# Normaliser rows stored as sixteen DRAM rows, with the step order, evacuation engines and buffers drawn up again

## Chip, cores and metric

The kernel runs on one core of a Trainium2 chip. The metric is the device time of one execution in microseconds; the figure for the kernel before is the median of three runs. The core has five engines with queues of their own: PE (matmul), DVE (vector), ACT (scalar and activation), POOL and SP, and 16 DMA engines that move data between DRAM and the on-chip memories.

## What is computed

Four residual layers over a sequence of 2048 rows of width 512 with 32 heads of 16: A, B, A, B, each on a layer-normalised copy of x. Both A layers use the same weights, and so do both B layers. Layer A is linear attention with a softmax feature map, layer B a sliding window of eight keys at distance two.

```python
def _A_ref(x, wqkv, w_phi, wo):
    qkv = ((x @ wqkv).reshape(B, S, 3, H, Dh)).transpose(2, 0, 3, 1, 4)
    q, k, v = qkv[0], qkv[1], qkv[2]
    pq = einsum("bhsd,hdf->bhsf", q, w_phi); pk = einsum("bhsd,hdf->bhsf", k, w_phi)
    phi_q = concat([softmax(pq), softmax(-pq)]); phi_k = concat([softmax(pk), softmax(-pk)])
    kv = einsum("bhsf,bhsd->bhfd", phi_k, v); z = einsum("bhsf->bhf", phi_k)
    o = einsum("bhqf,bhfd->bhqd", phi_q, kv) / (einsum("bhqf,bhf->bhq", phi_q, z)[..., None] + 1e-6)
    return merge_heads(o) @ wo
def _B_ref(x, wqkv, wo):
    # each query sees positions s, s-2, ..., s-14 (masked below 0)
    logits = einsum("bhsd,bhswd->bhsw", q, kg) * Dh ** -0.5
    o = einsum("bhsw,bhswd->bhsd", softmax(logits), vg)
    return merge_heads(o) @ wo
x = x + A(ln(x)); x = x + B(ln(x)); x = x + A(ln(x)); x = x + B(ln(x))
```

## The kernel before

The sequence is cut into four blocks of 512 rows (b = 0 to 3), each of four tiles of 128 rows. x stays on chip. For each of the two rounds L = 0, 1 and each block there is a chain of stages, and each stage is a method that registers small steps on named threads, one thread for each stage and engine.

- `s_loads`, `s_fold`, `s_ln_first`: loads of x and weights; w_phi is folded into the q and k parts of the A weights by transposes and matmuls whose PSUM results are copied into WA (`ev`, `ev2`); the first layer norm.
- `s_a1` (k and v of layer A): k projection on PE (L616 and L628 are the k and v matmuls), exponentials Ek on ACT (L622), sums and their reciprocal (t8 to t1 and `rr`), multiplication on DVE (L674), then `kv`, which adds up all blocks' key-value products in one PSUM bank.
- `s_a2` (q of layer A): projection (L721), exponentials Eq (L729), their sums S and 1/S.
- `s_akv`: the barrier. It needs the `kv` of all four blocks; it copies the sum to kvT and builds the matrices ZM and R from it.
- `s_a3`: the denominator from ZM and Eq, then the normaliser rho, a [128, 2, 128] tile that holds, for 4 tiles x 32 heads on the partitions, the two signs and 128 rows. rho must be spread over the 16 features of each head and multiplied into Eq. For four of the eight (round, block) pairs, (0,2), (0,3), (1,2) and (1,3), this goes through DRAM: `wr` stores rho (L847), `rdb` reads it back with repetition into Prho (L854), `muld` multiplies (L858). For the others PE spreads it (`bc`), and DVE multiplies from PSUM or from a bf16 copy that ACT makes (`bev`, L869; `mulp`, L839).
- `s_a4`: output of layer A and its projection; `s_out` adds the residual either on DVE (L556) or by an identity matmul on PE (L546) with a copy on ACT (L553), and does the sums and the layer norm that follows (L563, L575, L450 to L468; transposes by PE or by DMA, L473).
- `s_b1` to `s_b3` (layer B): projections (L950), `prod` of q and the shifted keys on DVE (L1042), head sums on PE (`lgt`, L1049), exponentials, sums and their reciprocal (`ex`, `den`, `rd`), the weights PT (L1077), the gathered v (`vrep`, DMAs Vg from V, L1011), `pav` on DVE (L1104), sums on PE (L1113) and the output projection (L543). The pair (1,3) takes another form of layer B, `s_e0` to `s_e4`, with its scores and outputs on PE (L1277, L1321, L1365), a mask product (L1303) and a normalisation oB on DVE (L1348).

The order of all steps on every engine is written out in three tables. `_ORDER` lists the threads in the order in which their next step is issued (base 36 numbers of thread names), 1488 entries; an engine executes its own steps in that order and waits by semaphores. `_CHOICE` has one digit for each movable step (an evacuation from PSUM, a normalisation, a residual add, a bf16 copy of spread rho): 1 is DVE and 0 is ACT, except that for a residual add 1 is PE with ACT, and for the copy of rho 1 means that there is none. `_SLOTS` says which buffer each tile takes: 16 medium ones, 8 PSUM banks, 8 large ones (Ek, prod, pav, Vg and others share them), 6 small ones.

```python
def copy(self, dve, out, in_):
    if dve:
        self.nc.vector.tensor_copy(out=out, in_=in_)   # L203
    else:
        self.nc.scalar.copy(out=out, in_=in_)          # L205
```

Of the kernel before, what the change touches and what calls it, by code (L numbers as in the profile page):

```python
# [8 lines left out]
BF16 = mybir.dt.bfloat16  # L9
# [7 lines left out]
P = 128  # L17
# [57 lines left out]
6k 6m 7s 6k 6n 6c 4v 69 6k 94 95 4x 96 97 6o 69 4x 6f 6i 98 6f 3h 6j 7t 7u 7w 6a 6e 6r 6r 6r 99 9a 99 99 9b 9c
9b 99 9d 9b 9e 6r 9b 9f 7y 7z 6q 6q 9b 83 9f 84 9j 6s 6s 9i 9g 6s 6s 88 6t 6t 9h 7y 80 b2 6s 6t 88 88 8b 4x 8a
6q 4x 4y 4y 7y 81 89 83 85 7y 8d 82 8f 6r 6u 9k 83 3h 4w 4x 9r 9s 9r 6u 6u 6q 4y 7x 88 9r 86 9t 9u 8c 9r 9v 6v
6w 6v 6u 6x 6v 6y 6v 9m 6z 70 70 9n 71 72 4w 73 70 70 83 74 9w 4v 72 72 4z 75 4z 72 50 4v 8e 50 51 8e 4z 50 53
4z 50 76 8f 72 52 76 54 79 9x 8f 87 9m 9m 55 55 55 55 7a 78 8f 77 7b 9o 56 57 8e 9w 9w 5a 9w 7x 58 57 9p 59 57
57 a1 a3 5b 9z 9y a3 57 5b 5e 5c 8g 8g 8g 8g a3 9m 9q 8h 8h 5f b3 b3 8e b3 a3 b4 5d 5g b6 8g 9l 8h b3 8f 8i bz  # L80
bz a4 a4 b5 a4 a4 b0 a0 a2 b7 a2 c0 c0 a5 a5 b1 b1 c0 c0 bz c0 b0 b1 a4 bx bx bx as as b1 by a5 at by by 8j by
8i 8j 8l 8i 8j 8m ar 8k 8i 8j 8n b0 b0 b1 8o a2 ap b1 8o 8o b1 b1 c0 a3 a6 by by 8p 8q a6 a6 8o 8r 8q 8s 8t ap
as 8q 8q 8u 8q a2 a6 8u 8w bz 8x ap a7 aq aq av a7 8y au a7 a8 b8 8v a7 b8 b8 a9 aa ap ab ac ac ac af ac c0 c0
ad as bx ag aq aq aq aq aq aq ae aw ah 8z bb bb b8 b9 bb by by ax be ax be b8 ae ae ae ai ae be be bc ai bc bc
aj ac ak ac am an ac ac bo bc bc ax ax ay bc al bb ao bc bm bn ax bc bj bm bn bn bn bm bn bn bp bu bu bu bu bq
bm bn bp bv bn br bg bj az az az az ba bj bj bu bk bz bu c0 bp bp bh c1 c1 c2 ba ba bf ba bj bl bl bu bu c1 c1
bl bu bi bl bw bs bt bw c2 bv bu bw bw c2 c2 c2 c2 c2 bx c7 c8 c9 c2 c1 c9 c9 ca fp by cb c2 cc cb c3 c4 c4 fq
fr ca cd c3 cg ce cb cb fq fs cf cb ca cj ch c3 c3 ci e0 c4 c4 cb cb cb cb ck cb c4 cl c4 c4 c4 e1 e2 cm cn e1
c3 c4 co e0 cp h9 e3 e1 ha e4 fs e1 cq e5 e1 e0 e8 e6 cq cq cr e9 cs e1 e7 e1 ea e1 e1 e1 hb ha fs cu hc ct cs
eb ee ed ec cs cq cv cs ef eg eh eg eg fq cw fq ft cs cw cy cx eg fu d1 fw cq cq cz ek d0 cq cq fv fx el fy fz  # L90
d2 ei ej ei ei ei em ei em eo fy hc eq ha ep df df df di df en da hc db dj ha dh dg d4 d5 dk d6 dl d5 d5 d8 hd
hg fy fy g3 da hf he hh hi da d7 dc hi hi da hi g2 g0 g1 dl g0 er g0 g0 hl g4 g0 dd hj ey ey ey hk hk hm de f8
ez dl et et hn g4 g6 f3 g5 hk d5 hk ho hk eu ho hq f3 hr et hp f3 dk hs dk g8 dk d9 f3 fa g7 f0 dl ev f1 f7 fa
f6 et f4 ey f5 f2 dm dm ew dm dm dn fb dn ht fb ex fa es i1 i2 i1 g9 i1 i4 dl dm i3 dn i1 i5 gl gl fb gn fa fb
i7 i9 i9 fc fc i9 id i9 fb gm ib fc ie f9 dl f9 gb gb ia gd hw hx c6 i6 do hu hu do do dp hv dq do gc dp i6 dp
dp i8 dt i6 i6 i6 gg i6 hw hw hz hy i6 i6 dr gb ge ds gg hw gi c6 i0 i6 i6 i6 i6 gg gj gg fa fd gk fe ff i6 i6
i6 i6 fd fe fg i7 if ig ic gh es ic ic gb f9 gf gq gs gs gs if ig if f9 if gl ig ig gl gp if if gt gt go ig ig
c5 c5 c5 gs gt gt gu gu if ig ih if ig ic ic ic ic ic du du dv ic gt gu du fd fd fe ih ih ih ic ic fh gs ic ic
# [14 lines left out]
_SLOTS = {  # L113
    "med": (
        "0123456789abcdef246559a55b68d5574c29efa8d2e9a857ef290d974caee2587fbd20897a5ecd5ddfbcee2dc7e456fb9a08"
        "e452d6f08c7ba4931e5fd62ca4"
    ),
    "ps": (
        "0123012456173526017417230146127631426134256126712307634256021304150236710245306712314025346710345267"
        "3012304562314023425671472345360123452102356174206345062306236231021341203145012301234524350123105423"  # L120
        "0452046312430567462306420316301452374523045014236570571057105270340123102345670123401567023451014265"
        "3012450120345670345012316750231720325674016237645701521342042042413510432034501256123120104523012020"
        "31220123012451302412"
    ),
    "big": (
        "012345670123451234567134056713052671054263754213675420137541036752034672046703154"
    ),
    "t2": (
        "0123455555555500112344444444444444444405012321222222224514031000010100011100002253333441000000000000"
        "000000025234113051"  # L130
    ),
    "pp": (
        "462462064646"
    ),
}

# [1 line left out]
class _Fast:  # L138
# [655 lines left out]
    def s_a3(self, L, b, dma):  # L794
        nc, add = self.nc, self.step
        st = "a3_%d%d" % (L, b)
        zm = self.ZM[L]
        T = {}
# [42 lines left out]
        pitch = (16 + _OPT["rho_pad"]) * P  # L841

        def wr():
            self.RD[L, b] = rd = self.dram.tile([8, 2, pitch], BF16, name="rd%d%d" % (L, b))
            a = rd[0:1, 0, 0:P]
            dst = bass.AP(a.tensor, a.offset, [[P, 16], [2 * pitch, 8], [pitch, 2], [1, P]])
            nc.sync.dma_start(out=dst, in_=T["rho"][:])  # L847

        def rdb(s):
            rd = self.RD[L, b]  # L850
            T["P", s] = pr = self.med([4, NB, P], "Prho")
            a = rd[0:1, s, 0:P]
            src = bass.AP(a.tensor, a.offset, [[2 * pitch, 8], [0, 16], [1, 16 * P]])
            nc.sync.dma_start(out=pr[:].rearrange("p t a i -> p (t a i)"), in_=src)  # L854

        def muld(s):
# [1243 lines left out]
```

## Time and profile before

| What | Value |
|---|---|
| Median of the runs (lowest to highest) | 333.31 us (331.84 to 334.52) |
| The profiled execution's own time | 333.73 us |
| Its span, first to last instruction | 332.0 us |
| Mean granted TensorE clock | 0.989 |
| Busy PE, DVE, ACT, POOL | 311.0, 291.6, 280.6, 42.0 us |
| HBM read and written | 11.13 MB, 2.99 MB |

The profile is of one execution. Busy time is the time in which an engine had an instruction in work; a row that groups instructions gives their number, their joint busy time and the mean duration of one, and after a second bar the idle time just before them with what ended it. Since instructions of one engine overlap a little, joint busy time over the number is less than the mean duration, and it is what one more instruction adds. A releaser in angle brackets is the work that ended a wait. "SPq" rows are DMA issues: the time is how long SP was held, not how long the data took.

### The profile page before, as it was taken

To read this page: it belongs to the slowest core of one execution; us is meant where nothing else is said; L and a number is where in the kernel's file an instruction comes from. 1 tells how busy PE (TensorE), PEld (TensorE's weight loads), DVE (VectorE), ACT (ScalarE), POOL (GpSimd) and SP (SyncE) were. 2 spreads that over 40 slices of the span, in tenths; PEclk is the share of its full clock that TensorE was granted. 3 is DMA by queue.
4 is the path that set the end of the run, shared out by engine and by line. 5 is a ranking of instruction groups with operands and counts; after the bars stand their busy time and mean duration, and the time that the engine had idled before them with its cause. 6 is when DMAs were issued, how large, how long until landed. Compare 5 with 4: busy or idle time off the path is not lost.

```text
span 332.0 us, 8893 instructions
## 1 busy us (share of the span) xinstructions
PE 311.0 (94%) x3551; PEld 153.6 (46%) x3577; DVE 291.6 (88%) x445; ACT 280.6 (85%) x648; POOL 42.0 (13%) x64
## 2 busy tenths in 40 slices
PE   8999999999999999899999999889999999996991
PEld 3654546445454443444443445644544444443540
DVE  5998996978999889999998899699699999998762
ACT  4899999998779998899999999999989858794640
POOL 7000000000205001040000000000001259440000
PEclk9999999999999999999999999999999999998997
DMA  7946200023889999569973000033399962779642
GB/s 201 363 116 126 88 0 4 2 60 88 162 130 157 132 163 146 85 120 159 140 100 58 8 2 4 4 88 103 84 119 149 183 141 51 186 132 158 112 160 72
DMA packets 44640, 36.14 MB, mean 109 GB/s; under 512 B 29680, under 2 KB 39984, under 8 KB 44592
## 3 DMA queue, kind: packets, MB, share of 16 engines
q1 hardware_dynamic: 44064, 35.48, 57.1%
q8 instruction: 30, 0.49, 0.7%
q14 instruction: 18, 0.15, 0.2%
q10 hardware_dynamic: 528, 0.02, 0.1%
HBM read 11.13 MB, written 2.99 MB: 43 GB/s over the span
## 4 chain that ended last, share of the span: by engine, by line
PE 33%; ACT 21%; DVE 12%; DMA 7%; issue 5%; SPq 1%; ACTq 0%; DVEq 0%
PE PS L950 13%; PE PS L543 7%; ACT Eq L729 5%; ACT sqd L563 4%; DMA Prho<-rd 3%; ACT Ek L622 3%; DVE prod L1042 3%; PE PS L1049 3%; PE PS L1170 2%; DVE pav L1104 2%; PE PS L1113 2%; DMA xnT<-xn 2%; DMA Vg<-V 2%; DVE Ek L674 2%; ACT oT L205 2%
## 5 line engine op out<-in xcount | busy, mean ns | idle before, releaser
L950 PE MATMUL PS<-xnT,WB 128*128 128x512 bf16 x336 | 77.3, 380 | 0.7 <-DVE QT L203 0.3
L1104 DVE TENSOR_TENSOR pav<-PT,Vg 128x4096 bf16<-128x4096 bf16 (+1 forms) x29 | 63.3, 2215 | 3.3 <-DMA Vg<-V 2.5
L1042 DVE TENSOR_TENSOR prod<-QT,K 128x4096 bf16<-128x4096 bf16 x28 | 63.2, 2286 | 0.3
L950 PEld LDWEIGHTS <-WB 128*128 128x128 bf16 x336 | 37.2, 114 | 37.5 <-issue 4.6
L543 PEld LDWEIGHTS <-oT 128*128 128x128 bf16 x240 | 22.4, 99 | 31.7 <-issue 6.2
L622 ACT ACTIVATE Ek<-PS 128x512 bf16<-128x512 f32 x64 | 34.0, 627 | 0.4 <-issue 0.4
L729 ACT ACTIVATE Eq<-PS 128x512 bf16<-128x512 f32 x64 | 34.2, 622 | 0.0
L563 ACT ACTIVATE sqd<-x 128x512 bf16<-128x512 bf16 x48 | 30.4, 634 | 3.9 <-DVE x L556 2.7
L992 POOL COPY vh<-V 128x64 bf16<-128x64 bf16 x6 | 9.6, 1592 | 180.4 <-ACT V L205 153.2
L543 PE MATMUL PS<-WoB,oT 128*128 128x512 bf16 x107 | 28.4, 390 | 3.6 <-issue 3.2
L205 ACT CAST oT<-PS 128x512 bf16<-128x512 f32 (+1 forms) x50 | 27.1, 594 | 4.7 <-PE PS L1113 4.6
L721 PE MATMUL PS<-xnT,WA 128*128 128x512 bf16 x128 | 30.6, 380 | 0.3 <-DVE Eq L839 0.3
L628 PE MATMUL PS<-WA,xnT 128*128 128x512 bf16 x123 | 30.5, 379 | 0.3
L543 PE MATMUL PS<-WoA,oT 128*128 128x512 bf16 x120 | 30.2, 379 | 0.5 <-issue 0.2
L616 PE MATMUL PS<-WA,xnT 128*128 128x512 bf16 x123 | 30.2, 379 | 0.3
L556 DVE SCALAR_TENSOR_TENSOR x<-PS,x 128x512 bf16<-128x512 f32 x42 | 27.2, 684 | 3.1 <-PE PS L543 2.9
L205 ACT CAST K<-PS 128x512 bf16<-128x512 f32 x31 | 17.6, 595 | 2.3 <-PE PS L1170 1.9
L628 PEld LDWEIGHTS <-xnT 128*128 128x128 bf16 x128 | 12.4, 98 | 14.7 <-issue 0.4
L674 DVE TENSOR_TENSOR Ek<-Ek,rk 128x4096 bf16<-128x4096 bf16 (+1 forms) x10 | 18.6, 1860 | 0.6 <-ACT rk L669 0.6
L616 PEld LDWEIGHTS <-xnT 128*128 128x128 bf16 x128 | 12.1, 98 | 15.1 <-issue 1.6
L553 ACT ACTIVATE x<-PS 128x512 bf16<-128x512 f32 x22 | 13.1, 601 | 6.5 <-PE PS L546 6.3
L721 PEld LDWEIGHTS <-WA 128*128 128x128 bf16 x128 | 11.8, 98 | 14.3 <-issue 0.6
(163 smaller groups left out, 509.9 us busy)
## 6 DMA issues: line engine op xcount, KB each, us to landing
Vg<-V SPq DMA_DIRECT2D x112, 131.5 KB, 5.7
Prho<-rd SPq DMA_DIRECT2D x8, 512.0 KB
x<-in_A_x_dram SPq DMA_DIRECT2D x3, 512.0 KB
WB<-in_B_wqkv_dram SPq DMA_DIRECT2D x3, 512.0 KB, 8.1
out_dram<-x SPq DMA_DIRECT2D x6, 256.0 KB, 3.1
wraw<-in_A_wqkv_dram SPq DMA_DIRECT2D x4, 256.0 KB
vd<-Vs SPq DMA_DIRECT2D x2, 272.0 KB, 4.3
x<-in_A_x_dram SPq DMA_DIRECT2D x4, 128.0 KB, 3.7
```

Source lines behind the costliest of these rows:

```text
L205: self.nc.scalar.copy(out=out, in_=in_)
L543: nc.tensor.matmul(y[:], lhsT=lh(t, c), rhs=Wo()[:, c, :], start=(c == 0), stop=(c == NB - 1 and not onpe))
L556: nc.vector.scalar_tensor_tensor(out=xb[:, t, :], in0=T[t][:], scalar=1.0, in1=xb[:, t, :], op0=ALU.mult, op1=ALU.add, **kw)
L563: nc.scalar.activation(out=sqd[:], in_=xb[:, t, :], func=ACT.Square, accum_out=T["ss"][:, t:t + 1])
L616: nc.tensor.matmul(pk[:], lhsT=xnT[:, t, k, :], rhs=self.WA[:, k, D:2 * D], start=(k == 0), stop=(k == NB - 1))
L622: nc.scalar.activation(out=T["E"][:, t, s, :], in_=T["k", t][:], func=ACT.Exp, scale=1.0 - 2.0 * s)
L628: nc.tensor.matmul(pv[:], lhsT=xnT[:, t, k, :], rhs=self.WA[:, k, 2 * D:3 * D], start=(k == 0), stop=(k == NB - 1))
L721: nc.tensor.matmul(pq[:], lhsT=self.WA[:, k, hb * P:(hb + 1) * P], rhs=xnT[:, :, k, :], start=(k == 0), stop=(k == NB - 1))
L729: nc.scalar.activation(out=self.Eq[L, b][s][:, :, hb, :], in_=T[hb][:].rearrange("p (t i) -> p t i", t=4), func=ACT.Exp, scale=1.0 - 2.0 * s)
L950: nc.tensor.matmul(pp[:], lhsT=self.WB[:, k, i * D + c:(i + 1) * D:NB], rhs=xnT[:, :, k, :], start=(k == 0), stop=(k == NB - 1))
L1042: nc.vector.tensor_tensor(out=pr[:], in0=QT[:, c:c + 1, :].to_broadcast([P, NW, TB]), in1=win, op=ALU.mult)
L1104: nc.vector.tensor_tensor(out=pv, in0=PT[:, :, lo:lo + n].unsqueeze(1).to_broadcast([P, NB, 2, n]), in1=vw, op=ALU.mult)
```

## The change

The code changes in one place, the stores and reads of rho. `wr` lays rho out in sixteen DRAM rows instead of eight, each of the two signs by a DMA of its own, and each value is stored in two rows; `rdb` reads sixteen rows, each eight times, where it read eight rows, each sixteen times.

```diff
         pitch = (16 + _OPT["rho_pad"]) * P
 
         def wr():
-            self.RD[L, b] = rd = self.dram.tile([8, 2, pitch], BF16, name="rd%d%d" % (L, b))
-            a = rd[0:1, 0, 0:P]
-            dst = bass.AP(a.tensor, a.offset, [[P, 16], [2 * pitch, 8], [pitch, 2], [1, P]])
-            nc.sync.dma_start(out=dst, in_=T["rho"][:])
+            self.RD[L, b] = rd = self.dram.tile([16, 2, pitch], BF16, name="rd%d%d" % (L, b))
+            for s in range(2):
+                a = rd[0:1, s, 0:P]
+                dst = bass.AP(a.tensor, a.offset, [[P, 16], [4 * pitch, 8], [2 * pitch, 2], [1, P]])
+                nc.sync.dma_start(out=dst, in_=T["rho"][:, s, :].unsqueeze(1).to_broadcast([P, 2, P]))
 
         def rdb(s):
             rd = self.RD[L, b]
             T["P", s] = pr = self.med([4, NB, P], "Prho")
             a = rd[0:1, s, 0:P]
-            src = bass.AP(a.tensor, a.offset, [[2 * pitch, 8], [0, 16], [1, 16 * P]])
+            src = bass.AP(a.tensor, a.offset, [[2 * pitch, 16], [0, 8], [1, 16 * P]])
             nc.sync.dma_start(out=pr[:].rearrange("p t a i -> p (t a i)"), in_=src)
 
         def muld(s):
```

The three tables are new. `_CHOICE` keeps the number of ones (120 of 380), at other places:

```diff
 _CHOICE = (
-    "1110110111101101111010000001100000000011000000101011111111101000001001110000000000000000100110101100"
-    "0001010100001111000000000000000011110001000000000111100000000000000011000111000000011011000000000000"
-    "1000000011111100000000000000110110100110110110111101000000000000000001010110011011001110001110100000"
-    "00000000011111010000011010000100000000000000000000000000010000011000000000001100"
+    "0010110111100111111111000000100000100110011100000111011110010100000101010000100000000000111101011100"
+    "1010010100001100100000000000000011111110000100001010100000000000000000010111001000001101000000000000"
+    "1010000011111100000000000100010110011011010100101111000000001001000000010110010001000100011100100000"
+    "00000000011111010000011100000000000000000000000001000011001000000000000000001100"
 )
```

Counted by kind, with the number on DVE before and after: evacuations of v in layer A 6 and 8, of layer A's output 10 and 12, of the key-value sum 0 and 1 (of 2), of layer B's projections 5 and 6, of the halo of k in the last block 0 and 1, of layer B's output 1 and 2, of first transposes 3 and 1; residual adds of layer A on DVE 26 and 29 (the rest on PE and ACT, 6 and 3); rho products straight from PSUM 21 and 18 of 32; normalisations 46 and 46 of 64.

`_ORDER` is another permutation of the same 1488 entries. Its first line before and after:

```diff
-4e d3 2 8 9 a b 0 d4 j 0 k i i i i i i 1m 1n i i i 2 1m 1o o i j l m i i i i 0 t 0 1m t 1m 1m 1m 3 p 3 1t 1t o f
+8 2e a d c 23 i i i 0 j 9 k j l i 2 i i i i 0 b o p i f 2 0 1m 1m 1o m n i i i i 1n 1m 1m 1p 1q 1m 1r o q r 1m t
...
```

Read by name, these are some of the differences. The first load is a tile of x rather than a part of the weights, the second block's x is loaded ahead of the q weights, and the B weights later. The first projection on PE is that of k rather than of v. In block (0,3) both reads of rho come behind the DMA transpose of block (0,1) on SP, where the first came ahead of it. Near the end, the fourth pav of block (1,1), two residual adds and two oB products come ahead of the PT of block (1,2) on DVE; on PE, two groups of L1321 come ahead of that block's `den`. The buffers of the gathered v of block (1,2) are those of its second and third `prod`, where they were those of the third and fourth.

More of the change, by code (lines that the diff above doesn't have):

```diff
@@ new lines @@
+4 z 1s s z i 3 1t 1u 21 z z 10 3 1t i7 1v 22 22 21 1 24 24 2p z 0 t u 13 11 15 1t 1t t 16 1w 1t 1y 12 12 12 12
+1x x 1t 5 v w w 25 y 14 2f 2f 18 18 18 18 1z 2g 2c 17 6 19 18 1c 1d 39 2d 1b 1a 2d 22 22 1f 1f g 21 22 22 3a 3a
+2c 2c 1f 2d 20 21 1f 22 2c 7 7 20 20 22 26 29 1g 1f 1k 39 3a 2d 2d 2d 2d 1i h 3b 2f 24 2i 1h 1e 29 1j 1l 2q 2h
+27 2d 2n 3c 2o 2o 29 29 2a 39 2k 2k 3a 2k 2k 2n 2n 2n 2q 2o 2o 2r 3a 3a 2q 2q 2o 2o 2o 29 2y 2y 2l 2s 2k 2o 2z
+2z 2z 2z 31 31 36 3c 33 24 36 36 28 36 2y 2y 2v 2v 2z 2v 37 36 2z 2z 2z 2f 2j 2u 2v 2b 2w 2b 2b 2b 2m 36 2m 36
@@ new lines @@
+7d 7g 63 4i 5z 91 4f 4n 4q 4q 4m 4q 63 66 67 64 65 7j 7i 7h 4l 7k 4r 93 4g 4g 4j 4w 4w 7l 7l 4o 4w 7o 68 4k 4q
+4u 93 93 4t 4s 4f 7l 7p 7m 7n 4p 4v 7n 7l 7q 6p 6k 6k 4v 6k 7n 7n 91 91 6f 6g 7r 6n 6m 6k 6a 6a 4w 94 6l 7n 69
+7r 7u 6o 7v 96 7t 97 4x 95 7s 7w 98 4x 4x 4x 6f 6c 6h 4y 4y 6a 6d 6b 6r 6r 99 6f 6i 6r 99 3h 99 99 9d 9e 3h 6f
+6j 6a 6e 9a 9b 9c 9b 6r 9b 9b 83 7y 7y 84 9f 9b 8d 7z 6s 6s 6s 9f 9h 6s 6t 6t 88 89 9i 7y 6s 6t 4w 4x 83 83 6q
+6q 7y 6q 85 88 4y 88 8b 83 9g 87 86 81 b2 9j 9k 88 8c 9m 9n 8f 9w 9x 82 9w 9w a1 6r 9z 69 6u 9w 80 6u 6v 8a 6u
@@ new lines @@
+6v 6x 6v 4w 6w 6q 6u 6v 6y 9m 4v 4z 4z 6z 4v 70 71 4z 4z 70 70 9y 72 7x 73 72 74 70 75 72 72 76 9o 9r 9r 50 51
+8f 50 50 72 52 76 78 8e 8e 50 53 77 54 9r 9u 79 7a 9m 9p 7b 8f 9s 9t 55 8e 56 57 8f 55 58 55 55 59 8g 8g 8g 8e
+a0 8g 57 57 a3 9r 5a 57 9v 9m 9q 5b a3 57 5b 8h 8h 5c b3 5e 5d 5f 5g 7x 9l a2 b0 b0 a3 b1 b1 b1 8g 8h b1 b3 b3
+b6 b3 b7 bz c0 c0 a4 a4 a4 a3 a4 a5 a5 bz c0 c0 bz d3 b4 bz c0 c0 c0 c0 8f 8i b0 b1 a4 8i 8i 8i a5 as at b0 b1
+b1 bx ap a2 b5 b1 ap 8j 8k 8j 8j 8l 8m 8j bx 8n 8o a3 a6 a2 a6 8p 8o 8o 8o bx aq aq aq aq by by by 8q 8t 8r 8s
@@ new lines @@
+as 8q a2 as as bx a6 a7 8q 8q a7 by 8u bz 8q a6 8u 8w 8y by by aw av 8v a7 8x a8 a7 aa ap ap a9 ab ac b8 b8 au
+ac i7 ac ac by by bx b8 b8 ad aq aq af aq aq ag b9 bo c0 8z ah b8 bb bb ae ae ae ae ai be ax ae ai aj an c1 be
+bc bb bc bc ak ax bc bb bc bc bc bc ac ac am ax ac ax ay al ac bg be bm bm ao bm bm bj bn bn bn bn bn bn ar ax
+az az az bu bu bu bu az bn bn c2 bv bj bj by bu bj bu ba ba ba ba bp bh bp bp c1 bq bk bs br be c1 c1 bu bu bu
+bp bj bf bl bl bl c2 c2 bi bl bv bw c2 c2 c2 bu bw c2 bw c2 bt bw c1 c7 c2 c8 c9 c9 ca c9 cb fp c3 cc cb ca ce
@@ new lines @@
+c4 c4 cf fq fr ca ch cg cj ck c3 c4 c4 cd cb cb ci cb c3 c3 fq fs fs cb cb cb c4 c4 c4 cb cb e0 e1 cl cm c4 c3
+e2 e1 e0 co e3 e1 cp cn cq e4 e1 e5 e0 e6 h9 c4 e1 e1 cq cq e8 e7 e1 e1 e9 e1 ea e1 eb cr cs ee ct ed cu ec ef
+fq cq fs fq ha cs cv cs cs cw eg eg ft fu hb ha hc fv eg eg hc hc fx fw fy fy cs cw cy cx d1 d0 fz ej cq cq cz
+eh g1 ei cq cq fy fy d2 df df df ei ek ei el ei em g3 dg ei em en d5 eq d6 g0 df dj da dh da d5 d5 d5 eo ep er
+g2 db ha di d4 d4 ha hd d7 dc d8 dl da da g0 he hh dl hg hf hi hi d9 g0 g0 g4 hi hi g0 de g4 g8 et et dk dk dk
@@ new lines @@
+hj hl et et dd hn es hm ev hk hk hk hk ho hk g6 g5 g7 g9 ho hq f3 f3 hr hs hp ht f4 f3 f3 f7 dl dl ey ey eu ez
+ex ey ey f8 fa dm dm dm dm ew f0 fa f6 f2 hu hv f5 es ga dn dn hw f1 dk i1 i2 i1 dl dm f9 f9 i3 c6 i6 i6 i6 hx
+hw hw dn hy fb i6 fa fb fa fb hz fb fc hu gl fc fb c5 fc gl dl do gn gl c6 dp do dp i1 i1 fa i6 i6 gb i8 i4 i9
+gc i9 i5 ib go ia i6 f9 f9 i9 i9 i6 do ie id gb i6 i6 i6 dr gm gg gh hw i0 gd gg gi ic ic dp ds dq do dp dt ic
+fd fe fd fe fd fg fe i6 i6 i6 i6 fh i6 c5 gb ge ic ff ic gg gj if ic ic if ic ic ic if ig ig gq gg gb gl gk gf
@@ L102 @@
+ig gs gs gs if if ig ig gp du if ig gs gt gt gt gt if gu ig if du du gu du dv ic c5 ic ic fd ih fe ih ih dy ig
+ih ic dz ic dw ii ii fi ij gr gr gt ij ik ij ij fj fj ik il ga gu il in gs fl ii ij ij gv ii fj fj im ij ij ik
+il ik fn fo gr gr il gw gx iq io iq iq gv gw gv gw gv gv ip iq iv dx dx fk fm fm gy gz h2 is gw gw ir it h2 iw
+iu h0 it ix iw h3 h3 h4 h5 h6 h2 h1 h3 h7 h2 h5 h3 h8 h5 h5
 """
 _CHOICE = (
[L106 removed]
```

66 lines of the change are left out of this document (16 added, 50 removed).

## The prediction

> **What bounds the kernel now.** I read the engines' totals first, then windows by stage, the timeline of the tail and the DMA share.
>
> ```profile
> span 332.0 us, 8893 instructions
> PE 311.0 (94%) x3551; PEld 153.6 (46%) x3577; DVE 291.6 (88%) x445; ACT 280.6 (85%) x648; POOL 42.0 (13%) x64
> ```
>
> PE is busy in all but 21 us of the span, so no order can gain more than that. The windows (columns: stretch, length, busy time of PE, PEld, DVE, ACT and POOL, granted clock, DMA share, GB/s) show where those 21 us are.
>
> ```profile
> 0.00:18.00 18.00, 16.35 (x121) 9.37 (x123) 13.49 (x41) 12.03 (x25) 6.32 (x36) 1.00 0.91 287
> 48.00:96.00 48.00, 46.48 (x720) 24.33 (x722) 42.38 (x93) 42.64 (x102) 2.08 (x3) 1.00 0.35 68
> 208.00:240.00 32.00, 29.23 (x561) 15.79 (x557) 25.44 (x61) 29.67 (x75) 0.00 (x0) 1.00 0.28 72
> 240.00:304.00 64.00, 61.65 (x693) 29.62 (x695) 62.50 (x63) 52.40 (x125) 23.51 (x13) 1.00 0.80 137
> 304.00:332.00 28.00, 19.20 (x287) 9.47 (x289) 15.06 (x22) 9.05 (x21) 0.24 (x1) 0.87 0.51 119
> ```
>
> They lie behind the two barriers at which all four blocks' key-value sums are needed (1.5 us in 48 to 96, 2.8 us in 208 to 240) and in the tail. From 240 to 304 DVE is busy 62.5 of 64 us: there it sets the pace beside PE. In the tail the last logits product ends on DVE at T = 293.84, PE pauses 3.17 us with no releaser, the PT product comes at 301.15, a pav product waits for its gathered V, and the last ACT evacuation starts at 322.30, 9.7 us before the span's end.
>
> ```profile
> 284.94 8.90 DVE L1042 TENSOR_TENSOR prod<-QT,K 128x4096 bf16<-128x4096 bf16 x4
> 301.15 0.68 DVE L1077 TENSOR_TENSOR PT<-E,rden 128x1024 bf16<-128x1024 bf16 x1
> 305.28 1.06 PE L543 MATMUL PS<-WoB,oT 128*128 128x512 bf16 x2 [3.17 <-issue]
> 307.17 2.29 DVE L1104 TENSOR_TENSOR pav<-PT,Vg 128x4096 bf16<-128x4096 bf16 x1 [1.35 <-DMA Vg<-V]
> 322.30 0.37 ACT L205 CAST oT<-PS 128x256 bf16<-128x256 f32 x1 [0.50 <-PE PS L1113]
> ```
>
> **Part 1, rho by sixteen rows.** The write becomes two DMAs a block, each holding SP 0.6 us, so the second half leaves 0.6 us later; its bytes double to 128 KB. The read-back keeps its bytes and its 4 KB runs; only the source's outermost count goes from 8 to 16.
>
> ```profile
> L847 SPq DMA_DIRECT2D rd<-rho x4: 582/592/606, 67.1 to 225.9; - x4
> 215.03 0.42 DVE L824 TENSOR_TENSOR rho<-rS,Ds 128x256 bf16<-128x256 f32 x1
> 217.98 1.39 SPq L854 DMA_DIRECT2D Prho<-rd  x2
> 219.00:220.00 1.00, 0.43 (x24) 0.30 (x12) 0.75 (x2) 0.97 (x4) 0.00 (x0) 1.00 0.29 66
> 222.00:223.00 1.00, 1.00 (x20) 0.43 (x19) 1.00 (x4) 0.95 (x3) 0.00 (x0) 1.00 0.61 131
> 227.00:228.00 1.00, 1.00 (x6) 0.48 (x6) 1.00 (x3) 1.00 (x4) 0.00 (x0) 1.00 0.42 78
> 89.00:90.00 1.00, 1.00 (x6) 0.43 (x5) 1.00 (x1) 1.00 (x3) 0.59 (x1) 1.00 1.08 273
> 97.88 1.23 DVE L858 TENSOR_TENSOR Eq<-Eq,Prho 128x2048 bf16<-128x2048 bf16 x1 [0.68 <-DMA Prho<-rd]
> ```
>
> Alone, the pair of reads (1 MB) runs at 131 GB/s on half of the DMA engines and takes about 8 us, 219.5 to 227.6. At 89 the queues together moved 273 GB/s with all engines. The pair's cost lies between 8 us (nothing gained) and 4 us (halved); I take 4, since the share is one half with a count of 8. [...]
>
> On the path this is worth little: DVE waited 0.68 us for a read, once, so the direct gain is 0 to 0.7 us and I take 0. The order spends it instead. From rho to the first multiply by it DVE has, adding its list at the rows' durations, 10.9, 17.4, 12.5 and 10.9 us of other work now, and 8.9, 11.4, 10.5 and 8.5 after (the second multiply 10.1 to 12.6). The chain needs 2.95 us from rho's start to the read's issue, 0.6 for the second write, 1.5 to first data and 2 us a read: 7.1 and 9.1 us. It fits, barely; one xnT transpose stands ahead of a pair of reads on SP in the second block.
>
> **Part 2, engines.** Counting the choices: eight PSUM evacuations (one of half width) go from ACT to DVE; three residual adds go from PE plus ACT to DVE; three rho products get a bf16 copy by ACT first; two xnT copies go from DVE to ACT; the normalisations come out even.
>
> ```profile
> L203 DVE CAST oT<-PS 128x512 bf16<-128x512 f32 x11 | 7.3, 684 | 0.0
> L205 ACT CAST oT<-PS 128x512 bf16<-128x512 f32 (+1 forms) x50 | 27.1, 594 | 4.7 <-PE PS L1113 4.6
> L556 DVE SCALAR_TENSOR_TENSOR x<-PS,x 128x512 bf16<-128x512 f32 x42 | 27.2, 684 | 3.1 <-PE PS L543 2.9
> L553 ACT ACTIVATE x<-PS 128x512 bf16<-128x512 f32 x22 | 13.1, 601 | 6.5 <-PE PS L546 6.3
> L546 PE MATMUL PS<-x,ident 128*128 128x512 bf16 x22 | 8.6, 390 | 0.0
> L839 DVE TENSOR_TENSOR Eq<-PS,Eq 128x512 bf16<-128x512 f32 x21 | 13.4, 682 | 0.0
> L839 DVE TENSOR_TENSOR Eq<-bs,Eq 128x512 bf16<-128x512 bf16 x11 | 4.2, 418 | 0.0
> L203 DVE COPY xnT<-PS 128x1024 bf16<-128x1024 bf16 (+1 forms) x7 | 4.4, 646 | 0.1
> L205 ACT COPY xnT<-PS 128x1024 bf16<-128x1024 bf16 (+1 forms) x4 | 3.6, 909 | 1.4 <-PE PS L482 1.4
> ```
>
> Busy time over count: DVE 7.5 x 0.66 + 3 x 0.65 - 3 x (0.64 - 0.38) - 2 x 0.63 = +4.9 us; ACT -7.5 x 0.54 - 3 x 0.60 + 3 x 0.54 + 2 x 0.9 = -2.4 us; PE -3 x 0.39 = -1.2 us at most. PE's gain counts only where PE alone paces; I take 0. DVE's 4.9 us are free where it idles (40 us in all) and on the path from 240 to T.
>
> **Part 3, order.** I added up, for each step of both lists, the work that its engine has ahead of it. Where PE's work up to a producer exceeds DVE's work ahead of the consumer, DVE must idle that much more than PE; the way back takes the margin off. Check on the kernel before: 6.1 - 4.4 = 1.7 us of PE idling at the first barrier (1.5 in 48 to 96) and 7.8 - 4.5 = 3.3 at the second (2.8 in 208 to 240). After: 6.2 - 3.6 = 2.6 and 4.8 - 2.1 = 2.7. So the first barrier costs +0.9 (0 to 1.5), the second about nothing, though its margin falls from 4.5 to 2.1.
>
> The start: folding is still paced by the raw weights and then by ACT's copies.
>
> ```profile
> 6.65 0.72 PEld L386 LDWEIGHTS <-wraw 128*128 128x128 bf16 x8 [1.00 <-DMA wraw<-in_A_wqkv_dram]
> 9.36 0.57 ACT L205 CAST WA<-PS 128x512 bf16<-128x512 f32 x1
> 11.23 1.89 PE L628 MATMUL PS<-WA,xnT 128*128 128x512 bf16 x7
> ```
>
> V's projection, which needs no folding, comes first now (11.23); after, K's comes first and waits for all four folded pieces, which ACT copies one after another, about 11.5. Walking PE's list with these rows leaves it 1.6 us behind at 18 us. ACT's list ahead of the barrier is 0.5 us shorter, which can take this up: +0.6 (0 to 1.6).
>
> From the second barrier to T, DVE's list grows from 79.5 to 82.9 us: one pav product and two residual adds come ahead of T, among smaller things. DVE idles 6.1 us of that stretch today (6.6 in 208 to 240, some 2 of it before the barrier's first DVE step, and 1.5 later). I let this take up some: +1.5 (0.3 to 3.4).
>
> The tail after T: 38.2 us now. After, DVE has a residual add, a pav, four masks, two adds and two oB products ahead of PT (8.6 us); PT's reciprocal stands behind two O matmul groups on PE, so PT comes near T + 10.5. Then PT, four pav and two oB (0.6 + 9.2 + 1.3) with 1 us of waiting end at T + 22.6, 0.4 for PE, and the last evacuation to the end 9.7: T + 32.7. The V gather can start one product earlier, since its first buffer is now the second product's, so the 1.35 us wait goes. If PE's pause recurs it now delays the den matmul ahead of PT: T + 35.9. So -5.5 to -2.3; the pause is as likely as not: -3.9. [...] The trace has a 3.17 us pause and does not name what it waited for.
>
> **The sum**, against the profiled execution's 333.73 us (0.4 above the median of 333.31): +0.6 + 0.9 + 1.5 - 3.9 + 0 = -0.9, so **332.8 us**; the bounds, with the 0.7 of the read, give 327.8 to 337.9 for this case.
>
> **Rivals.** *The tail opens fully*: no pause, DVE's idling absorbs the new work: 0.6 + 0 + 0.3 - 5.5 - 0.7 = -5.3, 328.4 us. For it: 240 to 304 is the only long stretch that DVE fills. Against: one trace cannot say whether the pause belongs to the order. *DVE paces from the second barrier on* (slower): its margin of 2.1 us is used up by the waits behind LayerNorm sums, PE then waits for each multiply by rho and each pav. It decides when DVE idles over 2.1 us more than PE after the barrier. Price: 0.6 + 0.9 + 3.4 + 2.4 (the lost margin) - 2.3 = +5.0, 338.7 us. For it: 82.9 us of DVE work in a stretch of 83.6. Against: ACT has 2.5 us less there. *The read stays at half rate*, as it would if the engines were picked by something else than the outermost count: the chain is 9.1 and 13.1 us, the second multiplies wait 3.0, 0.5, 1.4 and 2.8, 7.7 us of DVE, about half behind other stalls: +4, 336.8 us.
>
> **Chances.** The forecast 0.40, the open tail 0.25, DVE pacing 0.25, half rate 0.10. One per cent, 3.3 us, is about what a measurement of this kernel can tell from no change. Of the forecast's share 0.09 falls below 330.0, 0.24 within, 0.07 above 336.6; half rate splits 0.04 within and 0.06 above. So faster 0.34, same 0.28, slower 0.38. The range 326.5 to 340.5 covers the rivals with a little beyond; the forecast's own is 327.8 to 337.9.
>
> **What would show it.** Right: share near 1.0 and some 260 GB/s while Prho is read alone; rho to multiply about 9 us with DVE waiting under 1 us; DVE some 5 us busier; T near 297 and PT 10 us behind it; at most 33 to 36 us from T to the end. Wrong: a share of 0.5 there, PE idling over 4 us behind the second barrier, PE more than 3 us behind at 18 us, or T beyond 300.

## The result and the profile after

The changed kernel takes **329.0 us** (median of 20 runs, 327.2 to 330.67) against 333.55 us (20 runs, 331.01 to 335.13): a ratio of **0.9873, 95% interval 0.9853 to 0.9893**, 1.3% faster. The profiled execution has a span of 327.7 us against 332.0. The page's totals of the changed kernel (behind the change its line numbers are one higher than those of the kernel before):

```profile
span 327.7 us, 8877 instructions
PE 308.8 (94%) x3542; PEld 153.5 (47%) x3574; DVE 296.3 (90%) x456; ACT 278.1 (85%) x640; POOL 39.1 (12%) x64
```

DVE is 4.7 us busier, ACT 2.5 and PE 2.2 us less, against the counted +4.9, -2.4 and -1.2 at most (for PE, the two profiles of the kernel before differ by 1.3 us, 311.0 and 309.7). The windows of the changed kernel, with the columns of before:

```profile
0.00:18.00 18.00, 15.58 (x130) 9.68 (x133) 14.34 (x45) 13.11 (x26) 5.62 (x33) 1.00 0.93 266
48.00:96.00 48.00, 46.20 (x720) 24.43 (x722) 42.03 (x87) 42.63 (x101) 2.49 (x5) 1.00 0.31 73
96.00:168.00 72.00, 71.33 (x513) 32.80 (x519) 70.03 (x64) 67.76 (x158) 7.11 (x9) 1.00 0.87 136
208.00:240.00 32.00, 29.15 (x432) 14.82 (x436) 28.69 (x72) 28.94 (x71) 0.20 (x2) 1.00 0.34 84
240.00:304.00 64.00, 59.83 (x683) 28.46 (x688) 61.75 (x58) 49.96 (x117) 22.54 (x12) 0.99 0.85 142
```

The third of these stretches is one that the prediction did not quote. In the kernel before it reads:

```profile
96.00:168.00 72.00, 69.41 (x503) 31.32 (x508) 68.44 (x63) 67.11 (x155) 8.90 (x8) 1.00 0.94 137
```

PE idled 2.6 us of it and idles 0.7 now. Most of the unforeseen gain lies there. The rows that end the stages in the changed kernel, from the timeline (start, length, engine, line and, in brackets, idle time ahead and its releaser) and from the view of the tile `prod` (the last of its 28 starts at 290.9 and takes 2.28):

```profile
208.15 0.29 DVE L776 TENSOR_TENSOR ZM<-PS,maskH 128x32 bf16<-128x32 bf16 x2 [2.15 <-ACT rS L743]
302.03 0.69 DVE L1078 TENSOR_TENSOR PT<-E,rden 128x1024 bf16<-128x1024 bf16 x1 [0.35 <-ACT rden L1073]
302.62 1.43 PE L543 MATMUL PS<-WoB,oT 128*128 128x512 bf16 x4 [2.55 <-issue]
309.45 0.69 DVE L1349 TENSOR_TENSOR oB<-PS,rdB 128x512 bf16<-128x512 f32 x1 [4.41 <-ACT rdB L1341]
```

and the first of them in the kernel before (the others stand in the prediction):

```profile
210.24 0.29 DVE L776 TENSOR_TENSOR ZM<-PS,maskH 128x32 bf16<-128x32 bf16 x2 [1.93 <-ACT Eq L729]
```

`ZM` behind the first barrier moves from 53.8 to 54.3, behind the second from 210.24 to 208.15, T from 293.84 to 293.2, the end from 332.0 to 327.7. The read of rho is what it was meant to be (the windows in which it runs alone; in the kernel before, the windows of 222 to 227 have a share of 0.47 to 0.61 and 131 to 152 GB/s):

```profile
75.00:76.00 1.00, 1.00 (x14) 0.68 (x13) 1.00 (x5) 0.99 (x3) 0.00 (x0) 1.00 0.99 250
220.00:221.00 1.00, 1.00 (x44) 0.67 (x35) 1.00 (x3) 1.00 (x3) 0.00 (x0) 1.00 0.98 258
```

### The profile page after: what moved, and what is told of

Read it like the earlier page. It is cut to its first block, busy times and chain, and to the rows that moved or that the text cites. A ratio compares the mean times of both kernels' runs of the same rounds, so it can differ in the third digit from the quotient of the medians.

```text
span 327.7 us, 8877 instructions
## 1 busy us (share of the span) xinstructions
PE 308.8 (94%) x3542; PEld 153.5 (47%) x3574; DVE 296.3 (90%) x456; ACT 278.1 (85%) x640; POOL 39.1 (12%) x64
## 4 chain that ended last, share of the span: by engine, by line
DVE 31%; ACT 31%; PE 18%; issue 12%; DMA 3%; SPq 2%; DVEq 0%; ACTq 0%
DVE prod L1043 6%; ACT Eq L729 5%; DVE pav L1105 5%; PE PS L543 5%; ACT sqd L563 5%; ACT Ek L622 4%; DVE x L556 4%; DVE Ek L674 3%; PE PS L951 3%; DVE xn L466 3%; ACT oT L205 2%; PE PS L1050 2%; DVE s L649 2%; ACT xn L468 2%; DMA wraw<-in_A_wqkv_dram 1%
## 5 line engine op out<-in xcount | busy, mean ns | idle before, releaser
L543 PE MATMUL PS<-WoB,oT 128*128 128x512 bf16 x105 | 27.7, 393 | 3.1 <-issue 2.9
L616 PE MATMUL PS<-WA,xnT 128*128 128x512 bf16 x124 | 29.9, 379 | 0.5 <-DVE x L556 0.2
L628 PE MATMUL PS<-WA,xnT 128*128 128x512 bf16 x122 | 29.9, 379 | 0.3
L543 PE MATMUL PS<-WoA,oT 128*128 128x512 bf16 x119 | 29.3, 380 | 0.8 <-DVE x L556 0.2
L556 DVE SCALAR_TENSOR_TENSOR x<-PS,x 128x512 bf16<-128x512 f32 x45 | 28.9, 684 | 0.3 <-PE PS L543 0.2
L205 ACT CAST oT<-PS 128x512 bf16<-128x512 f32 (+1 forms) x47 | 24.8, 595 | 3.8 <-PE PS L1114 3.5
L205 ACT CAST V<-PS 128x512 bf16<-128x512 f32 x27 | 15.4, 591 | 4.1 <-PE PS L951 4.1
L466 DVE TENSOR_SCALAR xn<-x,rstd,nmr 128x512 bf16<-128x512 bf16 x46 | 16.8, 408 | 0.6
```

Of the source, the lines that this page charges most:

```text
L543: nc.tensor.matmul(y[:], lhsT=lh(t, c), rhs=Wo()[:, c, :], start=(c == 0), stop=(c == NB - 1 and not onpe))
L556: nc.vector.scalar_tensor_tensor(out=xb[:, t, :], in0=T[t][:], scalar=1.0, in1=xb[:, t, :], op0=ALU.mult, op1=ALU.add, **kw)
L616: nc.tensor.matmul(pk[:], lhsT=xnT[:, t, k, :], rhs=self.WA[:, k, D:2 * D], start=(k == 0), stop=(k == NB - 1))
L628: nc.tensor.matmul(pv[:], lhsT=xnT[:, t, k, :], rhs=self.WA[:, k, 2 * D:3 * D], start=(k == 0), stop=(k == NB - 1))
```

## The experiments

**Eight rows under the new order.** `rd` gets eight rows and one write a block again; tables stay the changed ones.

```diff
-            self.RD[L, b] = rd = self.dram.tile([16, 2, pitch], BF16, ...)
+            self.RD[L, b] = rd = self.dram.tile([8, 2, pitch], BF16, ...)
...
-            src = bass.AP(a.tensor, a.offset, [[2 * pitch, 16], [0, 8], [1, 16 * P]])
+            src = bass.AP(a.tensor, a.offset, [[2 * pitch, 8], [0, 16], [1, 16 * P]])
```

> The changed kernel with rho written to DRAM in eight rows as before; order, engines and buffers stay the changed ones. Theory 'rate' (the new order has only about 9 us between rho and the first multiply by it, and needs the read at full rate): the pair of reads takes 8 us again instead of 4.5, DVE waits for Prho in the second to fourth block of each layer, 1 to 4 us in all, and the time is 2 to 4 us above the changed kernel, 331 to 333. Theory 'order' (the read is hidden either way): the time stays within 0.8 us of the changed kernel, 328.2 to 329.8, and DVE's waits for Prho stay under 0.7 us.

Measured: **339.82 us**, ratio to the kernel before 1.0196 (1.0162 to 1.0231). "Rate" holds, at some three times its price. Its waits (engine, what it waited for: us in total, times, longest), and one of them in its timeline:

```profile
DVE Eq L858 <- DMA Prho<-rd: 10.7, 5, 6.1
PE PS L923 <- DVE Eq L858: 5.7, 4, 3.7
```
```profile
101.33 1.23 DVE L858 TENSOR_TENSOR Eq<-Eq,Prho 128x2048 bf16<-128x2048 bf16 x1 [6.07 <-DMA Prho<-rd]
```

In the changed kernel DVE never waits for `Prho`. DVE's waits are as much as the 10.5 us between the two spans (338.2 and 327.7): without the faster read the new order loses to the old one.

**Sixteen rows under the old order.** The diff of `wr` and `rdb` alone, on the tables of before.

> The kernel before with rho written in sixteen rows; nothing else changes. Theory 'rate': the share of the DMA engines while Prho is read alone goes from 0.5 to 1.0, the pair of reads from 8 to about 4.5 us, and since the read also holds up the V gathers behind it, part of the pav waits (1.6 us on PE before) goes too: 331.5 to 332.5, 1 to 2 us under the kernel before. Theory 'order': the read is faster but only the 0.7 us wait on DVE goes, and that not on the path: within 0.6 us of the kernel before, 333.0 to 334.1.

Measured: 333.61 us, ratio 1.0026 (0.9998 to 1.0055): "order" holds for the total. It was profiled once more, and so was the kernel before:

> The kernel before with rho in sixteen rows once more; its first profile was of its fastest execution (329.85 against a median of 333.61) and showed the second barrier's ZM at 208.2, not 210.2. Theory 'rate' for the middle (the faster read lets the V gathers start earlier): again near 208. Theory 'one execution': near 210, and pav waits over 2 us for Vg.

> The kernel before once more, to see which stages of its profile repeat. If the 2 us between the barriers are the order's: the second barrier's ZM comes near 210 again, with pav waiting over 2 us for Vg. If they belong to one execution: near 208.

They took 333.02 and 334.22 us. `ZM` of the second barrier came at 208.56 with sixteen rows and at 209.20 in the kernel before, both between the two values that the texts name, and pav waited 0.4 us for Vg there, not over 2. So the place of single waits changes between executions; what repeats is the time that PE idles. The same stretch of the kernel before in this second profile, then of the kernel with sixteen rows in its first and its second:

```profile
96.00:168.00 72.00, 69.91 (x506) 31.58 (x512) 69.13 (x63) 67.72 (x156) 8.12 (x8) 1.00 0.93 138
```
```profile
96.00:168.00 72.00, 71.14 (x512) 32.13 (x518) 70.29 (x63) 69.00 (x159) 8.42 (x8) 1.00 0.83 133
```
```profile
96.00:168.00 72.00, 71.15 (x512) 32.25 (x518) 70.17 (x66) 69.01 (x159) 8.42 (x8) 1.00 0.83 133
```

Both profiles with eight rows have 2.1 to 2.6 us of idle PE here, both with sixteen 0.9. In the kernel before, three of these waits read

```profile
124.90 2.29 DVE L1104 TENSOR_TENSOR pav<-PT,Vg 128x4096 bf16<-128x4096 bf16 x1 [1.17 <-DMA Vg<-V]
127.25 0.62 PE L1113 MATMUL PS<-pav,indAV 128*32 128x512 bf16 x8 [0.56 <-DVE pav L1104]
137.10 0.61 PE L1113 MATMUL PS<-pav,indAV 128*32 128x512 bf16 x8 [0.80 <-DVE pav L1104]
```

and with sixteen rows only one of 0.28 us is left:

```profile
135.42 0.61 PE L1114 MATMUL PS<-pav,indAV 128*32 128x512 bf16 x8 [0.28 <-DVE pav L1105]
```

How a read reaches these waits is seen on SP, which issues the gathers right behind it: SP is held 8.93 us by the first eight gathers (9.02 in the second profile) and 5.02 (5.01) with sixteen rows. First the kernel before, then sixteen rows:

```profile
89.41 8.93 SPq L1011 DMA_DIRECT2D Vg<-V  x8
```
```profile
89.29 5.02 SPq L1012 DMA_DIRECT2D Vg<-V  x8
```

The chain of work that ended last tells the same. In both profiles with eight rows it runs through the read ahead of these gathers, here that of the first profile (start, length; 9.69 us in the second); with sixteen rows no read of rho is among its 195 longest pieces:

```profile
88.04 9.82 DMA Prho<-rd
```

From barrier to barrier that is 156.4 and 155.7 us with eight rows, 154.4 twice with sixteen: 1.7 us, on the old order. "Rate" is right for this stretch. The total does not show it: 12 runs have the median of before. Where those 1.7 us go is open; the tail of the old order varies between profiles (36.4 to 39.7 us from T to the end over five of them), but the two profiles with sixteen rows fell on executions at or below their median (329.85 and 333.02), so they can't say what the other executions lost.

**Half of one order, half of the other.** Both with sixteen rows; the first has the old steps, engines and buffers up to the second barrier and the new ones behind it, the second the reverse.

```diff
 _ORDER / _CHOICE / _SLOTS
-  the changed kernel's throughout
+  h_ba: first 970 steps of before, then the rest in the changed kernel's order
+  h_ab: first 974 steps of the changed kernel, then the rest in before's order
```

> Rho in sixteen rows; the steps, engines and buffers of the kernel before up to the second barrier, those of the changed kernel behind it (13 buffers differ from both, since some were still in use). Theory 'by stages' (what the trace shows in each stage is worth as much when the other stages are the old ones): the stretch from the second barrier to the end gives +1.5 - 3.7 = -2.2 us, so 331.3, and the second barrier's ZM stays near 210. Theory 'one piece' (the tail or the middle profits only from where the other leaves its buffers and queues): within 0.8 us of one of the two kernels, 329 or 333.5.

> Rho in sixteen rows; the steps, engines and buffers of the changed kernel up to the second barrier, those of the kernel before behind it (14 buffers differ). Theory 'by stages': the stretch up to the second barrier gives +0.5 - 2.6 = -2.1 us, so 331.4, with ZM of the second barrier near 208 and a tail of 38 us from the last prod. Theory 'one piece': within 0.8 us of one of the two kernels.

Measured: 333.06 us (ratio 0.9998, 0.9973 to 1.0022) and 332.36 us (0.9979, 0.9957 to 1.0001). "By stages" falls: the halves give 0.0 and 0.7 us, not 2.2 and 2.1. "One piece" fits the first; the second lies 1.1 us under the 333.5 that it names, with an interval that reaches 1. In the first, by its one profile, the new tail is there (35.2 us) and the joint takes back what it gives: `ZM` of the second barrier, at 208.1 and 208.6 with sixteen rows on the old order, waits 3.38 us for ACT's `rS`, where in both whole orders it waits some 2.

```profile
210.03 0.29 DVE L776 TENSOR_TENSOR ZM<-PS,maskH 128x32 bf16<-128x32 bf16 x2 [3.38 <-ACT rS L743]
```

From there to T it takes 84.85 us, much as in the changed kernel (85.05), against 83.6 in the old order. In the second, ZM is early (207.7) and the old tail is back at 39.1 us.

**The old engine choices under the new order.**

```diff
-_CHOICE = ("0010110111100111111111000000100000100110...",)
+_CHOICE = ("1110110111101101111010000001100000000011...",)
```

> The changed kernel's order and sixteen rows with the engine choices of the kernel before (11 buffers differ): eight evacuations go back from DVE to ACT, three residual adds back to PE and ACT, three rho products back to a plain PSUM read. Theory 'engines count' (DVE's 4.9 us more work and ACT's 2.4 us less are in balance with the order): the steps queue behind a longer ACT and the time rises by 2 to 4 us, 331 to 333. Theory 'order alone': within 0.8 us of 329.

Measured: **363.1 us**, ratio 1.0893 (1.0836 to 1.095). "Engines count", but the 2 to 4 us expected were an order of magnitude short. The loss runs from the first barrier to T: from barrier to barrier it is 169.2 us instead of 153.9, from there to T 100 instead of 85; the tail is even shorter (32.3 us). The mean granted clock fell too, to 0.972 from 0.994. The longest waits of ACT and of DVE:

```profile
ACT oT L205 <- PE PS L1114: 9.9, 7, 4.4
...
DVE K L203 <- ACT Vs L205: 5.8, 1, 5.8
DVE prod L1043 <- ACT QT L205: 5.6, 2, 5.2
```

A step put on another engine stands there in front of what that engine's list was spaced for. So these choices and this order can't be parted; the buffers (11 differ here) were not varied alone.

**The tail: who sets the end?** Two pav products are put into DVE's wait of 4.41 us.

```diff
  DVE: PT pav(0)
-      oB(2) oB(3) pav(1) pav(2) pav(3)
+      pav(1) pav(2) oB(2) oB(3) pav(3)
```

> The changed kernel with the second and third pav product of block (1,2) ahead of the last two oB products on DVE, nothing else. DVE idles 4.41 us there for rdB. Theory 'DVE sets the end': two pav of 2.29 us fill that wait, the last pav starts about 4 us earlier, and with PE's work behind it the end comes 1.5 to 2.5 us earlier: 326.5 to 327.5. Theory 'PE sets the end' (PE is late from its 2.5 us pause and the half clock behind it, and has its O projections to do anyway): within 0.6 us of the changed kernel, about 329.

Measured: 329.07 us, ratio 0.9853 (0.981 to 0.9896): "PE sets the end". DVE finished its last pav early and then waited for PE:

```profile
302.33 1.02 PE L543 MATMUL PS<-WoB,oT 128*128 128x512 bf16 x4 [2.68 <-issue]
316.93 0.69 DVE L556 SCALAR_TENSOR_TENSOR x<-PS,x 128x512 bf16<-128x512 f32 x1 [4.32 <-PE PS L543]
```

From the pause on, PE has work almost without a break until its list ends (in the changed kernel it is busy 15.20 of the 15.38 us from 302.62 to 318.0); the pause is on the path. Three runs look for its cause.

```diff
  PE (tail_split): L1322(0)
-                  L1322(1) den
+                  den L1322(1)
  PE (mo_half):
-            for pos, n in ((0, 32), (32, 8)):
+            for pos, n in ((0, 32),):
  PE (split2):     L1322(0)
-                  L1322(1) den L543(0) L543(1) pt(0) pt(1) L1322(2) L1322(3) L543(2) L543(3) ...
+                  den L543(0) L543(1) L1322(1) pt(0) L543(2) pt(1) L543(3) L1322(2) pav(0) pt(2) L1322(3) ...
```

> The changed kernel with the den matmul and two O-projection groups put between the first two L1322 groups of 128 short matmuls (with the ln, rd steps that follow the second group moved behind it); nothing else. Theory 'code' (PE goes through 256 short instructions in 1.3 us and the code for what follows is not there yet while the gathers fill the DMA engines): the pause moves to behind the second group or shrinks by the 2 us put between, to under 1.5 us, and the time falls by 0 to 2 us. Theory 'clock' (the throttle stops PE after dense work): the pause keeps its 2.5 to 3.2 us and its place about 300, ahead of the second group. Theory 'DMA' (what follows waits for a transfer that the profile doesn't name): a pause of the same length in front of the same matmul.

The kernel that ran moved less than this text says: only the den matmul, 0.4 us, stands between the groups, the two O-projection groups do not. Measured: 328.8 us, ratio 0.9842 (0.9803 to 0.988), the pause unchanged in front of the same matmul. "Clock" loses its place for the pause; "code" and "DMA" are not told apart.

```profile
302.61 0.81 PE L543 MATMUL PS<-WoB,oT 128*128 128x512 bf16 x3 [2.53 <-issue]
308.04 0.21 PE L1322 MATMUL PS<-Vx,et 128*32 128x68 bf16 x2 [1.45 <-issue]
```

The second row is a pause that the changed kernel does not have, inside the third and fourth group.

> The changed kernel with the halo half of each L1322 group left out: 32 matmuls with their weight loads a group instead of 64, so the first two groups issue 128 instructions instead of 256 in a row (the window attention's neighbour part is missing from the output). Nothing is moved. Theory 'code' (PE runs out of code that is still being fetched while the gathers fill the DMA engines): the 2.5 us pause ahead of the first L543 matmul behind the groups falls under 1 us. Theory 'DMA' (that matmul waits for a transfer or an event that the profile does not name): the pause ends at the same time, about 302.6, so it gets longer by the 0.6 us that the groups save. Theory 'clock' (a stop after dense work): any length down to none, with the clock staying at 1.00 behind it.

Measured: 324.0 us (one run). Nothing is moved, the groups are half as long, and the pause is gone: the den matmuls run into the projections.

```profile
298.79 0.59 PE L1066 MATMUL PS<-E,indDen 128*128 128x512 bf16 x2
299.22 1.02 PE L543 MATMUL PS<-WoB,oT 128*128 128x512 bf16 x4
```

The same matmul starts 3.4 us earlier, T only 0.4 us, so it waited for no transfer that ends at 302.6: "DMA" falls.

> The changed kernel with other work between the four L1322 groups: den and two O-projection groups between the first and second, one transpose, two O-projection groups and another transpose between the second and third, a pav product's matmuls and a transpose between the third and fourth; PT and the first pav on DVE and den's reciprocal on ACT come earlier to fit (2 buffers differ). This is the spacing that tail_split missed: there only the den matmul went between. Theory 'code': the pause of 2.5 us falls under 1 us, PE, which is busy without a break from the pause to the end, ends 1.5 to 2.5 us earlier, 326.5 to 327.5. Theory 'DMA': the pause keeps its length in front of the first O projection and the time stays within 0.6 us of 329.

Measured: **327.34 us** (326.25 to 327.88), ratio 0.9804 (0.9759 to 0.9849), 1.7 us under the changed kernel and faster than both kernels of the case (the intervals of the two ratios do not overlap). The same instructions in another sequence; the longest pause by "issue" there is

```profile
301.84 0.20 PE L1322 MATMUL PS<-Vx,et 128*8 128x68 bf16 x2 [0.23 <-issue]
```

PE works as densely as before and nothing stops it, so "clock" falls too. Of the three theories "code" is left, and a line of the DMA view speaks for it: in the profiles a queue marked "instruction" moves blocks of 16 KB (30 packets, 0.49 MB in the changed kernel). The share below is of 16 engines for the stretch asked for, and packets are counted where they start. First the changed kernel, 299.6 to 299.8, then the kernel before, 301.8 to 302.0, then the second pause of tail_split, 305.0 to 305.2:

```profile
q8 instruction: 1, 0.02, 46.1%
```
```profile
q8 instruction: 1, 0.02, 47.6%
```
```profile
q8 instruction: 1, 0.02, 46.0%
```

46.1% of 16 engines for 0.2 us is 1.5 us of one engine: the block is on its way from 299.7 to 301.2, PE ran dry at 300.1 and goes on at 302.6. In the kernel before it starts 2 us later, and so does the pause. Under split2 it starts between 298.6 and 298.9, and PE is at long matmuls meanwhile. The packet times in the traces bear this out for all thirteen "issue" pauses of over 1 us in this part of the profiles: the pause begins between 1 us ahead of the block's start and 0.1 us behind its arrival and lasts 1.45 to 4.46 us, but PE went on each time 1.45 to 2.03 us after the block had arrived (changed kernel 301.15 and 302.62; tail_split's second 306.50 and 308.04; the longest, in the second profile of the kernel before, 303.53 and 305.54). Under split2 the block is there at 300.24 and PE has long matmuls until 301. That the queue is PE's is inferred: in the changed kernel, up to the tail, it moves a block for every 155 to 365 PE instructions (for ACT the numbers go from 9 to 55, for DVE from 4 to 36). The profile itself names no releaser, and what fills the 1.45 to 2.03 us behind the block is not shown.

Many short matmuls in a row were not enough. In the changed kernel the third and fourth group also run one behind the other (307.45 to 308.9) at a DMA share of 1.01, and PE's weight loads stop for 0.18 us only (308.36 to 308.54), its matmuls for 0.07: the next block had come at 306.88, and PE, at half clock until 306.5, was late. In tail_split PE gets there sooner and stops for the 1.45 us above.

**One step further**: the waits that split2 has left on DVE and PE.

```diff
  DVE (split3): PT pav(0) oB(1)
-               oB(2) pav(1) oB(3) pav(2)
+               pav(1) oB(2) oB(3) pav(2)
  PE (split3):  pav(0)
-               pt(2) L1322(3) ... pav(1)
+               L1322(3) pav(1) pt(2) ...
```

> split2 with the second pav product of block (1,2) ahead of the third oB product on DVE and the third pav product behind the fourth oB, and on PE the fourth L1322 group and the second pav product's matmuls ahead of the third transpose (3 buffers differ from the changed kernel). In split2 DVE waited 3.33 us for rdB and PE 1.6 us for oB. Theory 'DVE's wait was on the path': those PE waits go and the end comes 0.8 to 1.5 us earlier than split2, 326 to 326.5. Theory 'code': with the third and fourth group only 0.6 us apart again, PE runs out of code once more and a pause of 1 us or more comes back there: no gain, 327 to 328.5.

Measured: 328.03 us, ratio 0.9853 (0.9819 to 0.9886). No gain, and not for the reason given: the "issue" pauses stay under 0.25 us, but the fourth group shares a PSUM bank with the first pav product's sum, now stands right behind it, and waits for its evacuation.

```profile
310.18 0.21 PE L1322 MATMUL PS<-WA,et 128*32 128x68 bf16 x2 [1.64 <-ACT oT L205]
```

## Why the prediction was right or wrong

Against the profiled execution the terms were, forecast and measured: up to the first barrier +0.6 and +0.5; from the first barrier to the second +0.9 and **-2.6**; from there to T +1.5 and +1.5; the tail -3.9 and -3.7. The sum was -0.9 and came out -4.3. The time lies inside the range, near its fast end: the forecast gave 0.34 to a time below 330.0 and 0.38 to a slower kernel; three of four terms come close, one of them by luck (the tail, below), and one has the wrong sign.

**The term that failed** is the middle, in two steps of Part 1 and Part 3. "The direct gain is 0 to 0.7 us and I take 0": the price of the slow read was taken from the one row in which DVE waited for `Prho`. But a read also held up the V gathers that SP issues next (8.93 us for eight of them, 5.02 with the faster read), and part of its cost was booked under other names: pav waiting for `Vg`, PE waiting for pav. The chain of work that ended last, in the same profile, had shown it: 9.82 us of it are one read. Taking the read alone away (sixteen rows, old order) shortens this stretch by 1.7 us. The other step is the first barrier's "+0.9": PE idles 1.8 us of 48 to 96 against 1.5, so +0.3. Some 0.5 us between the barriers is the new order's own, and part of the 2.6 belongs to the one execution: the second profile of the kernel before has 155.7 us here and not 156.4.

**The rho chain** ("it fits, barely") was right, and the run with eight rows shows how barely. The forecast priced that rival at +4 us against its sum, 336.8; it measured 339.82, since one block pays 6.07 us at once. The half rate itself is out: the share is 0.98 at sixteen rows against 0.47 to 0.61 at eight, by the same bytes and runs. With the rows alone changed, on the old order, it is 0.96 to 1.01 (218 to 221). When the prediction was made, no run had shown a share at sixteen rows, and the 4 us for a pair of reads was an estimate from the half share at eight; in the changed kernel the second round's first pair moves its data in 4.7 us (217.1 to 221.8), where the kernel before takes 8.0 (219.4 to 227.4).

**DVE's 4.9 us** were there and were not the bound: from the second barrier to T came +1.5 as forecast, and the rival in which DVE paces from the second barrier is out, with PE idling 2.85 us in 208 to 240, under the 4 us named. The argument for that rival, 82.9 us of DVE work in a stretch of 83.6, counted rows' durations, and these overlap: in busy time DVE has 77.5 us before and 80.2 us in 85.05 now, so there was more room. T itself lies at 293.2 and not near 297, since the middle had gained before.

**The tail.** PT came at T + 8.8 (forecast 10.5), the gather's wait of 1.35 us is gone, and the end is T + 34.5 (forecast 34.3, between 32.7 without and 35.9 with the pause). That -3.7 stands so near to -3.9 is luck. The forecast is the mean of two cases, and neither came: it put the pause ahead of the den matmul, where it would delay PT, and the pause came behind it. It also added the tail up along DVE's list, and PE sets the end: with DVE's last pav done some 5 us earlier (tail_pav2, 312.6 instead of 317.8) the time stays at 329.07 us. The pause is in every profile of these orders that keeps the first two groups at full length with at most the den matmul between them, eleven in all, 2.3 to 4.5 us, so even odds were too low for it. What PE waits for in the pause, the forecast left open; the 16 KB block of the instruction queue, on its way from 299.7 to 301.2 in the changed kernel, is what the runs point to.

The rival *the tail opens fully* (328.4 us) lies nearer to the median than the forecast, but not by its mechanism: the pause stayed, and the gain that it looked for in the tail came between the barriers.

## What to carry to other kernels

Price a slow transfer by taking it away, not by the waits that bear its name: here what stood behind it in its queue paid under other names (SP was held 8.93 us by eight gathers against 5.02), and the chain that ended last named it. The order drawn up with the faster transfer was worth nothing without it (339.82 us against 333.55). An order and its engine choices are one plan here: parts of two good plans gave next to nothing, and one plan's order with the other's choices lost 34 us. Where PE stands still by "issue" behind hundreds of very short matmuls, look for a block of the instruction queue at that time, and spread the matmuls among long ones (329.0 to 327.34 us here).

## What the runs showed of the hardware

PE stopped for 2.3 to 4.5 us behind 256 short instructions (1.41 us of PE in the changed kernel, 1.94 in the kernel before), while a 16 KB block of the instruction queue was moved in 1.2 to 1.5 us at a DMA share of 0.8 to 1.1 (1.48 us at 1.04 and 1.52 us at 1.08 in these two); with 128 instructions there (mo_half), or with longer matmuls between (split2, longest pause 0.23 us), it did not stop. No run changes the load of the DMA engines, so whether the pause needs them busy is open.

After the stop of 2.55 us in the changed kernel the granted clock fell to 0.50:

```profile
302.00:304.00 2.00, 1.38 (x5) 0.58 (x5) 1.94 (x2) 0.00 (x0) 0.00 (x0) 0.78 1.04 156
304.00:306.00 2.00, 2.00 (x7) 0.59 (x4) 1.04 (x1) 0.00 (x0) 0.00 (x0) 0.50 1.05 164
```

In tail_split, with a pause of 2.53 us at the same place, it stays at 1.00, and so does the first of the half-and-half kernels behind 2.96 us.

```profile
302.00:304.00 2.00, 1.39 (x7) 0.77 (x8) 1.82 (x2) 0.11 (x2) 0.00 (x0) 1.00 1.05 158
304.00:306.00 2.00, 2.00 (x74) 1.46 (x72) 1.16 (x1) 0.08 (x1) 0.00 (x0) 1.00 1.06 170
```

In split2, where PE did not stop, it is 1.00 as well:

```profile
304.00:306.00 2.00, 1.93 (x33) 0.95 (x37) 0.02 (x1) 0.59 (x1) 0.00 (x0) 1.00 1.05 174
```

In the changed kernel the clock stands at 0.50 for 3.41 us (303.11 to 306.52) and then at 1.00 for 20.48 (to 327.00), six times as long; in the kernel before it does so for the same times (304.22 to 307.63, to 328.11). Cut into steps of 3.41 us, the eight profiles in which the pause is followed by 0.50 had PE busy for 0.12 to 1.43 us of the step that the pause fell into (0.86 in the changed kernel, 299.70 to 303.11), and those that stayed at 1.00 for 1.68 us or more (1.72 in tail_split, 300.92 to 304.33; 1.79 and 1.68 in the half-and-half kernel and the one with the old choices). Nothing was measured between. So the pause of 2.55 us in the changed kernel cost more than its length: matmuls of 0.38 us took 0.63 in the 3.41 us at 0.50.
